# Operand places, turned maxima and the order of unfilled steps in an attention and MLP kernel

## The chip, the cores and the metric

The kernel runs on one core of a Trainium2 chip. The metric is the time of one execution in microseconds as the device reports it; lower is better. Before the change it is 1652.32 us, the median of three runs from 1651.63 to 1653.09.

A core has TensorE (matrix products, PE in the profile, with its weight loads as PEld), VectorE (DVE), ScalarE (ACT), GpSimd (POOL) and SyncE (SP, whose queue issues most of the DMAs). Each engine works through its own queue in order, and semaphores tie the queues together.

## The reference

One transformer block of 2048 rows and width 512, with adaptive layer norms. The attention has 32 heads of width 16, which share one key and one value head; the MLP has 1376 hidden columns. Cut to what matters:

```python
mod = (silu(c) @ w_mod).reshape(1, 6, 1, -1)          # sa, ca, ga, sb, cb, gb
h = layernorm(x) * (1 + ca) + sa
q = (h @ wq) as 32 heads;  k = h @ wk;  v = h @ wv
p = softmax(q @ k.T * 16 ** -0.5)                      # for each head
x = x + ga * (concat(p @ v) @ wo)
h = layernorm(x) * (1 + cb) + sb
x = x + gb * (gelu(h @ w1 + b1) @ w2 + b2)
```

## The kernel before

**Numbers.** Most products are float32r. To keep float32 accuracy, an operand is split into a high part and a low part (the rest), and a product is made of three: high by high, low by high, high by low. The helper `split` makes the parts, `mm3` and `batches` list the three products.

**Units and steps.** The rows are cut into eight blocks of 256, the heads into eight groups of four. A block and a group make a unit; there are 64. The keys are gone through 256 at a time: eight steps K for each unit. In a step, for the four heads of the unit,

- `Max.step` (L452) makes a score product m of 128 query rows by 512 keys, and VectorE reduces it to its maximum (L465). This runs about six steps ahead of the rest;
- `sexp` (L503) makes a score product e with keys on the rows. The maxima stand as two extra rows (48 and 49 of each half of qst, high and low part), so that the product has the maximum subtracted, and ScalarE takes the exponential into p (L516);
- `pv` (L518) multiplies p with the values and a column of ones into acc (L527), in four column tiles of the array at once.

The products m and e contract over 64 rows, so two run side by side, one in each half of the array: half s has rows 64 s to 64 s + 63.

**The maxima of a unit.** When the last m of a unit is reduced, VectorE reduces the four key chunks to mm, 128 rows by 8 (L473). Two quarters later `put_max` (L478) turns mm with a transpose on TensorE into the PSUM tile mt (L485), ScalarE copies it out (L489), GpSimd splits it into mh and ml, and two quarters after that four DMAs of SP put them into the rows of qst (L496).

**The order of the work** is written out by hand. Steps go in pairs X and Y, and a counter `clock` advances four quarters for each pair; `later(n, fn)` runs something n quarters on. Between the score products of a pair the kernel puts a batch of other products where one is ready (`take`): late query projections (qps), the output projection (wops), transposes (tp), the MLP (w1ps, w2ps). Its 64-row halves run in the half of the array that the scores leave free. A step with a batch is called filled here. Without a batch `plain` (L1248) issues the step alone, half of the m and e for each array half; `mixture` alternates two lists, and `issue` merges lists by their lengths. The loop is at L1230.

PSUM has eight banks: three for m, one each for e0, e1, e2, one (v) for acc, and one (x) for the batches.

```python
free = ((1, 2, 0, 1), (2, 0, 1, 2)) if holder else ((1, 2, 0, "x"), (1, 2, 0, "x"))
plain(1, X, 0, (n + 2) // 4, free[0])
```

The four numbers are the banks of the step's four e; `holder` is a batch job that still holds x.

**The late shift and scale columns.** The modulation rows for the second layer norm are made in the prologue as rows of a PSUM tile. `late_mods` (L873) sends two of them (ga, gb) to DRAM and back as rows for all partitions, and turns the two others (sb, cb) into columns with four TensorE transposes and two VectorE copies (L902 to L906).

**Places in SBUF.** `pad` (L84) allocates a small tile and zeroes it on GpSimd, so that what is allocated behind it lies further on. With the pads of this version, the operands of all float32r products start at multiples of 128 bytes in their partition: ks, qst, wqH, wqL, bigH, bigL, woH, woL, gH, gL, w1t and the tiles tagged xH and xL.

**The tail.** The last block's MLP has no attention beside it and uses the whole array (`fast`). `stir` (L680) issues products on ks there, whose result nobody reads, while the layer norm is made.

Of the kernel before, what the change touches and what calls it, by code (L numbers as in the profile page):

```python
# [15 lines left out]
P = 128  # L16
# [7 lines left out]
LEAD_0 = 3  # L24
QBUFS = 4
# [8 lines left out]
STIR = (4, 8, 4)  # L34
# [7 lines left out]
def adaln_mqa_mlp(  # L42
# [158 lines left out]
    xts = []  # L201

# [6 lines left out]
    pad(pro, 480, "pad1")  # L209
# [41 lines left out]
    pad(pro, 480, "pad2")  # L251
# [49 lines left out]

    wqH = att.tile([P, KD, D], F32R, name="wqH", tag="gH")
# [12 lines left out]
    hts_stats = {}  # L315
    bigH = att.tile([P, NB - 1, KD, BQ], F32R, name="bigH", tag="bigH")
# [4 lines left out]

    tps = {}
# [109 lines left out]
    class Max:  # L432
# [5 lines left out]
        def begin(self, u):  # L438
            T = blocks[units[u][0]][1] // P
            items = [(j, t, kc) for j in range(2) for t in range(T) for kc in range(NKC)]  # L440
            if u == 0:
                items.sort(key=lambda a: a[2])
            self.items[u] = [list(items), list(items)]
            self.left[u] = 2 * len(items)
            self.mx[u] = att.tile([P, 4 * T, NKC], F32, name=f"mx{u}", tag="mx", bufs=2)
            if u == 0:
                pad(att, 192, "pad3")
# [4 lines left out]
        def step(self, s):  # L452
# [9 lines left out]
            nc.tensor.matmul(m, qsts[u][rows, j, t * P:(t + 1) * P], ks[rows, kc * 512:(kc + 1) * 512],  # L462
                             start=True, stop=True)
            i = (s * 2 + j) * T + t
            nc.vector.tensor_reduce(out=self.mx[u][:, i, kc:kc + 1], in_=m, axis=AX.X, op=ALU.max)  # L465
            self.done += 1
            self.left[u] -= 1
            if self.left[u] == size[u] // 2 and u and u + 1 < NU:
                load_q(u + 1)
            if self.left[u] == 0:  # L470
                put_at[u] = clock[0] + 2
                mm = att.tile([P, 4 * T], F32, name=f"mm{u}", tag="mm", bufs=2)
                nc.vector.tensor_reduce(out=mm, in_=self.mx.pop(u), axis=AX.X, op=ALU.max)  # L473
                maxima[u] = mm

    maxima = {}

    def put_max(u):  # L478

        w = blocks[units[u][0]][1]  # L480
        T = w // P
        qst = qsts[u]
        mm = maxima.pop(u)
        pt = psum.tile([P, 512], F32, name=f"mt{u}", tag="m", bufs=3)
        nc.tensor.transpose(pt[:4 * T, :P], mm, ident)  # L485
        mh = att.tile([4 * T, P], F32R, name=f"mh{u}", tag="mh", bufs=2)
        ml = att.tile([4 * T, P], F32R, name=f"ml{u}", tag="ml", bufs=2)
        m32 = att.tile([4 * T, P], F32, name=f"m32_{u}", tag="m32", bufs=2)
        nc.scalar.copy(m32, pt[:4 * T, :P])  # L489
# [13 lines left out]
    def sexp(u, K, j, s, bank):  # L503

        w = blocks[units[u][0]][1]
        qst = qsts[u]
        if (u, K) not in ptiles:
# [7 lines left out]
        nc.tensor.matmul(e, ks[rows, kt * P:(kt + 1) * P], rhs, start=True, stop=True)  # L515
        nc.scalar.activation(ptiles[u, K][:, j, s, :], e, AF.Exp, scale=0.25)  # L516
# [163 lines left out]
    def stir(n):  # L680

        ps = psum.tile([P, BQ], F32, name=f"stir{len(idles)}", tag="x")
        idles.append(ps)
        for _ in range(n):
            nc.tensor.matmul(ps, ks[:, 0:P], ks[:, 0:BQ], start=True, stop=True)

    def rest_steps(b, fast, rp, bank, ons, ready):
# [6 lines left out]
        for hf in range(w // HQ):  # L694
# [37 lines left out]
            for t in range(2):  # L732
# [3 lines left out]
                if fast:  # L736
                    add_x(t, ps)
                    stats(t)
                    rstd(t, t + 1)
                    xhat(t)  # L740
                else:
                    add_x(t, ps)
                    later(2, lambda t=t: stats(t))
            if not fast:
                later(3, lambda: rstd(0, 2))
                later(4, lambda: xhat(0))
                later(4, lambda: xhat(1))
                yield 7
# [120 lines left out]
    drm = tc.dram_tile([2, D], F32, name="drm")  # L869
# [3 lines left out]
    def late_mods():  # L873
# [10 lines left out]
        def spread():  # L884
            nc.sync.dma_start(out=drm[0:1, :], in_=rows[0:1, :])
            nc.sync.dma_start(out=drm[1:2, :], in_=rows[96:97, :])
            later(3, collect)

        def collect():
            nc.sync.dma_start(out=ga, in_=drm[0:1, :].to_broadcast([P, D]))  # L890
            nc.sync.dma_start(out=gb, in_=drm[1:2, :].to_broadcast([P, D]))
            later(4, scale)

        def scale():
            nc.gpsimd.tensor_tensor(out=b2g, in0=b2r, in1=gb, op=ALU.mult)
# [4 lines left out]
        yield 4  # L900
        psc = psum.tile([P, KD, P], F32, name="modlc", tag="x")
        mod_cols(psc, rows, P)  # L902

        def cols():
            nc.vector.tensor_copy(out=sb, in_=psc[:, :, 32])
            nc.vector.tensor_scalar(out=cb1, in0=psc[:, :, 64], scalar1=1.0, scalar2=None, op0=ALU.add)  # L906

        yield 0
        cols()
# [29 lines left out]
    def prep_w1():  # L939
# [10 lines left out]
        def work(f):  # L950
            w1s[f] = rp.tile([P, 2, KD, P], F32R, name=f"w1s{f}", tag="w1t", bufs=3)
# [63 lines left out]
    put_at = {}  # L1015
# [162 lines left out]
    def put_some():  # L1178
        for u in sorted(maxima):
            if clock[0] >= put_at[u]:  # L1180
                put_max(u)

    while mp.done < lead[0]:
        if mp.done % 4 == 0:
            due()
            put_some()
# [7 lines left out]
    for u in sorted(maxima):  # L1194
        put_max(u)
# [24 lines left out]
    def end_step(u, K):  # L1220

        pv(u, K)
        put_some()
# [6 lines left out]
    for u in range(NU):  # L1230
        for K in range(0, steps[u], 2):
# [16 lines left out]
            def plain(s, K, t, n, banks):  # L1248

                a, b_, c_, d = banks  # L1250
                one = mixture(maxes(s, n), exps(s, [(K, 0, a), (K, 1, c_)]))
                other = maxes(t, n)
                issue(one, other[:1] + exps(t, [(K, 0, b_), (K, 1, d)]) + other[1:])
# [9 lines left out]
            else:  # L1263
                free = ((1, 2, 0, 1), (2, 0, 1, 2)) if holder else ((1, 2, 0, "x"), (1, 2, 0, "x"))
                plain(1, X, 0, (n + 2) // 4, free[0])
# [10 lines left out]
            else:  # L1276
                plain(1, Y, 0, n // 4, free[1])
# [68 lines left out]
```

## Time and profile before

| what | value |
|---|---|
| median of three runs | 1652.32 us (1651.63 to 1653.09) |
| profiled execution | 1652.47 us, its span 1650.6 us |
| TensorE products busy | 1613.0 us, 98% of the span |
| VectorE busy | 1418.4 us, 86% |
| ScalarE busy | 1222.8 us, 74% |
| GpSimd busy | 609.6 us, 37% |
| granted TensorE clock, mean | 0.997 |
| DMA | 22.3% of 16 engines for SP's queue |

The span is the time from the first to the last instruction in the trace. Busy time is the time in which an engine had at least one instruction running. TensorE's products overlap each other, so a product's own duration (about 0.39 us for 512 columns) is longer than the pitch at which products follow each other; where the text speaks of a pitch, it is the distance from start to start. In a row of groups the order is: line, engine, operation, out<-in with shapes, count, then busy us and mean ns of one, then the idle time of the engine just before and what ended it. In a timeline row it is: start in us, duration in us, engine, line, operation, tiles, count of merged instructions.

### The profile page before, as it was taken

The numbers are of one execution on the slowest core, as the hardware profiler recorded it, in microseconds if no ns is written. First come the engines' busy times: TensorE is split into PE (matmuls) and PEld (weight loads), VectorE is DVE, ScalarE is ACT, GpSimd is POOL, SyncE is SP. The second block draws the span as 40 slices with busy tenths as digits, with TensorE's granted clock in tenths as the row PEclk, the third lists the DMA queues.
The fourth block names the chain that finished last, engine by engine and source line by source line (L and its number), as shares of the span: only waits on it lengthen the run. The fifth ranks groups of instructions, "written<-read, shape, count | busy, mean of one in ns | idle before, by whom it ended". The sixth has DMA issues, their size and how long they took to land.

```text
span 1650.6 us, 41339 instructions
## 1 busy us (share of the span) xinstructions
PE 1613.0 (98%) x16387; PEld 1031.3 (62%) x16387; DVE 1418.4 (86%) x2433; ACT 1222.8 (74%) x2445; POOL 609.6 (37%) x898
## 2 busy tenths in 40 slices
PE   6999999999999999999999999999999999999998
PEld 4455644456666576656766576656766576656767
DVE  7688999999988998899988998899988998899625
ACT  4356777778877787778877787778877788778843
POOL 6235246424601363124601363124601364124613
PEclk9999999999999999999999999999999999999999
DMA  7234321212112030212112030122212030122232
GB/s 262 81 116 157 136 74 54 81 43 79 57 48 76 26 108 15 63 59 82 54 42 81 30 106 17 51 71 71 65 33 88 21 115 18 47 82 68 71 114 86
DMA packets 80157, 121.61 MB, mean 74 GB/s; under 512 B 15496, under 2 KB 53000, under 8 KB 79964
## 3 DMA queue, kind: packets, MB, share of 16 engines
q1 hardware_dynamic: 79852, 118.96, 22.3%
q8 instruction: 130, 2.13, 0.5%
q14 instruction: 63, 0.52, 0.1%
q0 software_dynamic: 112, 0.01, 0.0%
HBM read 91.13 MB, written 27.26 MB: 72 GB/s over the span
## 4 chain that ended last, share of the span: by engine, by line
PE 85%; DVE 9%; issue 2%; ACT 1%; POOL 1%; DMA 1%; SPq 1%; DVEq 0%; POOLq 0%; ACTq 0%
PE acc L527 29%; PE m L462 25%; PE e L515 14%; PE w1ps L177 6%; DVE mx L465 6%; PE w2ps L177 3%; PE wops L177 1%; PE w2ps L171 1%; PE w1ps L171 1%; ACT p L516 1%; PE mt L485 1%; PE kps L153 1%; PE qps L177 1%; PE tp L177 1%; DVE st L716 1%
## 5 line engine op out<-in xcount | busy, mean ns | idle before, releaser
L465 DVE TENSOR_REDUCE mx<-m 128x1 f32<-128x512 f32 x2048 | 1278.8, 682 | 150.1 <-PE m L462 121.9
L516 ACT ACTIVATE p<-e 128x512 f32<-128x512 f32 x2048 | 1071.3, 599 | 295.4 <-PE e L515 228.1
L462 PE MATMUL m<-ks,qst 64*128 64x512 f32 x2048 | 838.2, 433 | 12.1 <-DVE mx L465 4.1
L515 PE MATMUL e<-qst,ks 64*128 64x512 f32 x2048 | 704.1, 399 | 2.7 <-DMA qst<-ml 2.6
L527 PE MATMUL acc<-p,va 128*32 128x256 f32 x8192 | 548.0, 385 | 0.0
L462 PEld LDWEIGHTS m<-ks,qst 64*128 64x128 f32 x2048 | 358.7, 183 | 274.2 <-DVE mx L465 183.2
L515 PEld LDWEIGHTS e<-qst,ks 64*128 64x128 f32 x2048 | 359.6, 185 | 43.2 <-ACT p L516 19.1
L527 PEld LDWEIGHTS acc<-p,va 128*32 128x32 f32 x8192 | 213.8, 109 | 218.9 <-issue 117.1
L177 PE MATMUL w1ps<-h2H,w1t 64*128 64x256 f32 x1232 | 240.8, 290 | 0.0
L177 PEld LDWEIGHTS w1ps<-h2H,w1t 64*128 64x128 f32 x1232 | 186.5, 186 | 0.0
L123 POOL TENSOR_SCALAR mh<-m 8x128 fp32r<-8x128 f32 x64 | 18.5, 289 | 453.0 <-ACT m L489 446.0
L177 PE MATMUL w1ps<-h2L,w1t 64*128 64x256 f32 x616 | 171.8, 279 | 0.0
L177 PE MATMUL w2ps<-w2L,gH 64*128 64x512 f32 x282 | 115.7, 410 | 0.0
L177 PE MATMUL w2ps<-w2H,gH 64*128 64x512 f32 x282 | 115.5, 410 | 0.0
L177 PE MATMUL w2ps<-w2H,gL 64*128 64x512 f32 x282 | 115.5, 410 | 0.0
L177 PEld LDWEIGHTS w1ps<-h2L,w1t 64*128 64x128 f32 x616 | 114.8, 186 | 0.0
L811 POOL TENSOR_SCALAR tt<-tt 128x256 f32<-128x256 f32 x77 | 31.2, 405 | 179.6 <-DVE mx L465 98.5
L128 POOL TENSOR_TENSOR gL<-z,gH 128x256 fp32r<-128x256 f32 x88 | 66.3, 753 | 18.2 <-DVE gH L127 11.8
L812 POOL TENSOR_TENSOR tt<-tt,z 128x256 f32<-128x256 f32 x77 | 56.9, 739 | 6.4
L822 POOL TENSOR_TENSOR z<-tt,z 128x256 f32<-128x256 f32 x77 | 56.1, 729 | 6.0
L821 POOL TENSOR_TENSOR tt<-tt,z 128x256 f32<-128x256 f32 x77 | 56.2, 730 | 0.0
L177 PEld LDWEIGHTS w2ps<-w2H,gH 64*128 64x128 f32 x282 | 51.9, 184 | 0.6
(186 smaller groups left out, 1445.8 us busy)
## 6 DMA issues: line engine op xcount, KB each, us to landing
w1t<-dw SPq DMA_DIRECT2D x82, 512.0 KB
qst<-dq SPq DMA_DIRECT2D x384, 32.0 KB
do<-oc SPq DMA_DIRECT2D x64, 128.0 KB
dw<-w1s SPq DMA_DIRECT2D x11, 512.0 KB
xt<-in_A_x_dram SPq DMA_DIRECT2D x4, 1024.0 KB
wml<-in_w_mod_dram SPq DMA_DIRECT2D x8, 512.0 KB
dq<-qH SPq DMA_DIRECT2D x16, 256.0 KB
dq<-qL SPq DMA_DIRECT2D x16, 256.0 KB
```

The costliest lines, as they stand in the source:

```text
L128: eng_l.tensor_tensor(out=dst_l, in0=src, in1=raw(dst_h), op=ALU.subtract)
L171: nc.tensor.matmul(ps, a, b_, start=first_, stop=last_)
L177: nc.tensor.matmul(ps, a[rows], b_[rows], start=first_ and s == 0, stop=last_ and s == 1)
L462: nc.tensor.matmul(m, qsts[u][rows, j, t * P:(t + 1) * P], ks[rows, kc * 512:(kc + 1) * 512], start=True, stop=True)
L465: nc.vector.tensor_reduce(out=self.mx[u][:, i, kc:kc + 1], in_=m, axis=AX.X, op=ALU.max)
L515: nc.tensor.matmul(e, ks[rows, kt * P:(kt + 1) * P], rhs, start=True, stop=True)
L516: nc.scalar.activation(ptiles[u, K][:, j, s, :], e, AF.Exp, scale=0.25)
L527: nc.tensor.matmul(accs[u][32 * cidx:32 * cidx + 32, :], va[:, kt, :], rhs, start=kt == 0, stop=kt == NKT - 1)
L811: nc.gpsimd.tensor_scalar(out=tt, in0=tt, scalar1=1.0, scalar2=1.0, op0=ALU.mult, op1=ALU.add)
L812: nc.gpsimd.tensor_tensor(out=tt, in0=tt, in1=z, op=ALU.mult)
L821: nc.gpsimd.tensor_tensor(out=tt, in0=tt, in1=z, op=ALU.mult)
L822: nc.gpsimd.tensor_tensor(out=z, in0=tt, in1=z, op=ALU.add)
```

## The change

- **Places.** Pads of 64 bytes go before xt and p (and with them qst), before wqH, before bigH, before the tiles xH and xL, and before w1t. After that, in each float32r product, one operand starts at a multiple of 128 bytes and the other 64 bytes past one. Two later pads keep what follows in place.
- **Maxima.** `put_max` runs at once when a unit's last m is reduced. VectorE reduces into one of two fixed tiles of 128 by 32 (zeroed once) and turns it in 32 by 32 blocks. One quarter later GpSimd copies the four pieces of 8 by 32 into mt, 8 by 128, and splits it; four quarters after the maximum the four DMAs are issued. The transpose on TensorE and ScalarE's copy are gone.
- **Order.** In an unfilled step, e goes first in both halves, and the fourth m is written to the bank x where no batch holds it. The four e use only e0 to e2, so that the fourth has the bank of the first.
- **Columns.** sb and cb go to DRAM as rows and come back as columns by DMA, with GpSimd adding one. The four transposes and two copies of `late_mods`, and its two waits, are gone.
- **Smaller.** In the blocks that are not the last, the layer norm's statistics and what follows run one quarter later. `stir` issues the same number of products, with the moving operand starting at columns 0, 4, 8 and so on.

```diff
-STIR = (4, 8, 4)
+STIR = ((0, 0, 0, 0), (0, 4, 8, 12, 16, 20, 24, 28), (16, 32, 48, 0))
+MAX_WAIT = (1, 4)
...
+    pad(att, 64, "pad1")
     def load_x(b):
...
+    pad(att, 64, "pad4")
     wqH = att.tile([P, KD, D], F32R, name="wqH", tag="gH")
...
+    pad(att, 64, "pad5")
     bigH = att.tile([P, NB - 1, KD, BQ], F32R, name="bigH", tag="bigH")
...
+    pad(att, 64, "pad6")
     tps = {}
...
-            m = psum.tile([P, 512], F32, name=f"m{u}_{j}_{t}_{kc}_{s}", tag="m", bufs=3)
+            m = psum.tile([P, 512], F32, name=f"m{u}_{j}_{t}_{kc}_{s}", **(place or dict(tag="m", bufs=3)))
...
             if self.left[u] == 0:
-                put_at[u] = clock[0] + 2
-                mm = att.tile([P, 4 * T], F32, name=f"mm{u}", tag="mm", bufs=2)
-                nc.vector.tensor_reduce(out=mm, in_=self.mx.pop(u), axis=AX.X, op=ALU.max)
-                maxima[u] = mm
+                put_max(u, self.mx.pop(u))
...
-        pt = psum.tile([P, 512], F32, name=f"mt{u}", tag="m", bufs=3)
-        nc.tensor.transpose(pt[:4 * T, :P], mm, ident)
...
-        nc.scalar.copy(m32, pt[:4 * T, :P])
-        split(mh, ml, m32, nc.gpsimd, nc.gpsimd)
+        nc.vector.tensor_reduce(out=mm[:, :4 * T], in_=mx, axis=AX.X, op=ALU.max)
+        turned = att.tile([P, 32], F32, name=f"turned{u}", tag="turned", bufs=2)
+        nc.vector.transpose(out=turned, in_=mm)
+        mt = att.tile([4 * T, P], F32, name=f"mt{u}", tag="mt", bufs=2)
...
-        later(2, send)
+        def gather():
+            for g in range(0, P, 32):
+                nc.gpsimd.tensor_scalar(out=mt[:, g:g + 32], in0=turned[g:g + 4 * T, :], scalar1=1.0, scalar2=0.0,
+                                        op0=ALU.mult, op1=ALU.add)
+            split(mh, ml, mt, nc.gpsimd, nc.gpsimd)
+
+        later(MAX_WAIT[0], gather)
+        later(MAX_WAIT[1], send)
...
         def spread():
             nc.sync.dma_start(out=drm[0:1, :], in_=rows[0:1, :])
             nc.sync.dma_start(out=drm[1:2, :], in_=rows[96:97, :])
+            nc.sync.dma_start(out=drm[2:3, :], in_=rows[32:33, :])
+            nc.sync.dma_start(out=drm[3:4, :], in_=rows[64:65, :])
...
+                nc.sync.dma_start(out=sb, in_=drm[2].rearrange("(k p) -> p k", p=P))
+                nc.sync.dma_start(out=cb1, in_=drm[3].rearrange("(k p) -> p k", p=P))
...
-        psc = psum.tile([P, KD, P], F32, name="modlc", tag="x")
-        mod_cols(psc, rows, P)
...
+            if f == 0:
+                pad(rp, 64, "pad8")
...
-                one = mixture(maxes(s, n), exps(s, [(K, 0, a), (K, 1, c_)]))
+                one = mixture(exps(s, [(K, 0, a), (K, 1, c_)]), maxes(s, n))
                 other = maxes(t, n)
-                issue(one, other[:1] + exps(t, [(K, 0, b_), (K, 1, d)]) + other[1:])
+                if not holder and mp.has(t) and n > 1:
+                    other[-1] = 1.0, lambda: mp.step(t, tag="x", bufs=1)
+                issue(one, exps(t, [(K, 0, b_)]) + other + exps(t, [(K, 1, d)]))
...
-                free = ((1, 2, 0, 1), (2, 0, 1, 2)) if holder else ((1, 2, 0, "x"), (1, 2, 0, "x"))
-                plain(1, X, 0, (n + 2) // 4, free[0])
+                plain(1, X, 0, (n + 2) // 4, (1, 2, 0, 1))
...
-                    later(2, lambda t=t: stats(t))
+                    later(3, lambda t=t: stats(t))
```

More of the change, by code (lines that the diff above doesn't have):

```diff
@@ L506, in sexp @@
         qst = qsts[u]
+        assert u in placed
         if (u, K) not in ptiles:
@@ L678, in fetch_rest, with stir @@
         early[b] = x1, w1ts
-    def stir(n):
+    def stir(starts):
         ps = psum.tile([P, BQ], F32, name=f"stir{len(idles)}", tag="x")
         idles.append(ps)
-        for _ in range(n):
-            nc.tensor.matmul(ps, ks[:, 0:P], ks[:, 0:BQ], start=True, stop=True)
+        for i in starts:
+            nc.tensor.matmul(ps, ks[:, 0:P], ks[:, i:i + BQ], start=True, stop=True)
     def rest_steps(b, fast, rp, bank, ons, ready):
@@ L742, in rest_steps @@
                     add_x(t, ps)
-                    later(2, lambda t=t: stats(t))
+                    later(3, lambda t=t: stats(t))
             if not fast:
[L745 to L748, printed above, removed]
+                later(4, lambda: rstd(0, 2))
+                later(5, lambda: xhat(0))
+                later(5, lambda: xhat(1))
+                yield 8
             hH = att.tile([P, KD, HQ], F32R, name=f"h2H{b}_{hf}", tag="xH", bufs=2)
@@ L1193, in adaln_mqa_mlp @@
             clock[0] += 1
-    for u in sorted(maxima):
-        put_max(u)
     preps["w1"] = prep_w1()
```

45 lines of the change are left out of this document (19 added, 26 removed).

## The prediction

> **What bounds the kernel now.** I read the page first: the busy shares, the chain that ended last, the dearest groups.
>
> ```profile
> span 1650.6 us, 41339 instructions
> PE 1613.0 (98%) x16387; PEld 1031.3 (62%) x16387; DVE 1418.4 (86%) x2433; ACT 1222.8 (74%) x2445; POOL 609.6 (37%) x898
> PE 85%; DVE 9%; issue 2%; ACT 1%; POOL 1%; DMA 1%; SPq 1%; DVEq 0%; POOLq 0%; ACTq 0%
> L465 DVE TENSOR_REDUCE mx<-m 128x1 f32<-128x512 f32 x2048 | 1278.8, 682 | 150.1 <-PE m L462 121.9
> L516 ACT ACTIVATE p<-e 128x512 f32<-128x512 f32 x2048 | 1071.3, 599 | 295.4 <-PE e L515 228.1
> ```
>
> TensorE carries 85% of the chain. VectorE, second, is idle mostly because it waits for m: it follows TensorE, not the reverse. The profiled execution took 1652.47 us (1.9 around its span of 1650.6), beside a median of 1652.32, so the sum below holds for the median too.
>
> The attention loop has 64 units of eight key steps, and 512 steps fill nearly the whole span. There are two kinds. A filled step carries a batch of projection or MLP products on one half of the array while the other half does m and e. An unfilled one has m and e alone. How many there are follows from the groups, with shapes kept apart:
>
> ```profile
> L177 PE MATMUL w1ps<-h2H,w1t 64*128 64x256 f32 x1232 | 240.8, 290 | 0.0
> L177 PE MATMUL w1ps<-h2L,w1t 64*128 64x256 f32 x616 | 171.8, 279 | 0.0
> L177 PE MATMUL w2ps<-w2L,gH 64*128 64x512 f32 x282 | 115.7, 410 | 0.0
> L177 PE MATMUL wops<-woL,onH 64*128 64x512 f32 x112 | 43.8, 391 | 0.0
> L177 PE MATMUL tp<-ident,xh 64*128 64x128 f32 x224 | 32.1, 284 | 0.0
> L177 PE MATMUL qps<-bigL,wqH 64*128 64x512 f32 x72 | 28.3, 393 | 0.0
> ```
>
> A w1 step has 12 half products: 1848 / 12 = 154 steps. The w2, wo and qps rows stand three times each (high·high, low·high, high·low): 846 / 5.5 = 154, 336 / 6 = 56, 216 / 6 = 36. tp has eight records a step: 28. That is 428 filled steps, and 84 unfilled.
>
> One filled step, TensorE in order of time (start, us, and what; the rows left out alternate m and e, with w1 products between):
>
> ```profile
> 800.79 1.07 PE L527 MATMUL acc<-p,va 128*32 128x256 f32 x16
> 801.79 0.49 PE L462 MATMUL m<-ks,qst 64*128 64x512 f32 x1
> ...
> 802.13 0.39 PE L515 MATMUL e<-qst,ks 64*128 64x512 f32 x1
> ...
> 803.29 0.42 PE L462 MATMUL m<-ks,qst 64*128 64x512 f32 x1
> ...
> 803.65 1.07 PE L527 MATMUL acc<-p,va 128*32 128x256 f32 x16
> ```
>
> The step takes 803.65 − 800.79 = 2.86 us: 1.00 for acc, 0.34 to the second product, five pitches of (803.29 − 802.13) / 5 = 0.232, and 0.36 until acc can start. No gap waits for anything: this step is as long as its products' pitch makes it.
>
> An unfilled stretch, TensorE, then VectorE and ScalarE in the same stretch:
>
> ```profile
> 250.85 1.07 PE L527 MATMUL acc<-p,va 128*32 128x256 f32 x16
> 251.85 0.27 PE L485 MATMUL mt<-ident,mm 128*8 128x128 f32 x1
> 252.06 0.66 PE L462 MATMUL m<-ks,qst 64*128 64x512 f32 x2
> ...
> 253.76 1.07 PE L527 MATMUL acc<-p,va 128*32 128x256 f32 x16
> 254.77 0.50 PE L462 MATMUL m<-ks,qst 64*128 64x512 f32 x2
> 255.10 0.39 PE L515 MATMUL e<-qst,ks 64*128 64x512 f32 x2
> ...
> 256.05 0.50 PE L462 MATMUL m<-ks,qst 64*128 64x512 f32 x1
> 256.48 1.07 PE L527 MATMUL acc<-p,va 128*32 128x256 f32 x16
> ```
>
> ```profile
> 255.30 2.48 DVE L465 TENSOR_REDUCE mx<-m 128x1 f32<-128x512 f32 x4 [0.23 <-PE m L462]
> ```
>
> ```profile
> 255.53 2.07 ACT L516 ACTIVATE p<-e 128x512 f32<-128x512 f32 x4 [0.64 <-PE e L515]
> ```
>
> Here the step is 256.48 − 253.76 = 2.72, although it has far less to do. m has three PSUM buffers, so its fourth product waits for the first reduction: 255.30 + 0.68 = 255.98, and m starts at 256.05. Only then can acc go. VectorE's own need is smaller: four reductions take 2.48, a pitch of (2.48 − 0.68) / 3 = 0.60, so 2.40 a step.
>
> **The change, part by part.**
>
> *The turned maxima.* Removed from TensorE: 64 transposes mt. From acc to the next m it is 252.06 − 250.85 = 1.21 with one and 254.77 − 253.76 = 1.01 without: 0.20 each, on the chain in both kinds of step. 64 × 0.20 = 12.8; I take 12, since the first lies in the prologue and a little may return. VectorE gets a 32x32-block transpose of 128x32, in its queue right behind the last reduction. Nearest row:
>
> ```profile
> L473 DVE TENSOR_REDUCE mm<-mx 128x8 f32<-128x32 f32 x64 | 11.9, 186 | 2.2
> L123 POOL TENSOR_SCALAR mh<-m 8x128 fp32r<-8x128 f32 x64 | 18.5, 289 | 453.0 <-ACT m L489 446.0
> L128 POOL TENSOR_TENSOR ml<-m,mh 8x128 fp32r<-8x128 f32 x64 | 29.0, 452 | 5.3
> ```
>
> About 0.19, 12 us in all, covered by VectorE's idle 0.23 before a step's m. Without that cover it would be up to 0.19 × 64 = 12 and the saving would be gone; what queues behind it are the next reductions, for which TensorE's next m waits. ScalarE loses a small copy each time. GpSimd gets four copies of 8x32, each at most 0.29 by the mh row: 1.16 more a unit, 74 us on top of 609.6 of 1650.6, off the chain. Should GpSimd be late, the sends of the rows wait in SP's queue, and everything SP issues behind them. The gather is issued one quarter of a step pair after the maximum (before: at the end of a later step), the four sends four quarters after it, about one quarter earlier than now. They pass no load that a product needs at once; priced at 0. mm now comes from two fixed tiles, zeroed once.
>
> *Order of unfilled steps.* e goes first, and the last m takes a fourth buffer, x, where no batch holds it. Then no m waits. But the fourth e now reuses the bank of the first e, and waits for its exponential. A first product after acc reaches its reader 255.30 − 254.77 = 0.53 later; the exponential is 0.60, the restart 0.07: 1.20, against 256.05 − 254.77 = 1.28 now. 0.08 × 84 = 7 us. Bounds: VectorE's 2.40 would allow 2.72 − 2.40 = 0.32 × 84 = 27; and 0, or a small loss, if ScalarE has an oc copy or a tanh in front. I take 7, because the new wait is a row of the same stretch.
>
> *The 64 bytes.* In the layout of before, both operands of every fp32r product start at a multiple of 128 bytes. Five pads of 64 bytes put one of the two at 64. No fp32r product in this trace lies otherwise, so the rows can only bound it. From the tail, whole array, no waits:
>
> ```profile
> 1596.12 0.39 PE L171 MATMUL w2ps<-w2L,gH 128*128 128x512 f32 x1
> ...
> 1602.92 0.39 PE L171 MATMUL w2ps<-w2L,gH 128*128 128x512 f32 x1
> ...
> 1609.50 0.60 PE L769 MATMUL tp<-ident,xh 128*128 128x128 f32 x4
> ```
>
> ```profile
> 1617.39 0.28 PE L171 MATMUL w1ps<-h2L,w1t 128*128 128x256 f32 x1
> ...
> 1621.70 0.28 PE L171 MATMUL w1ps<-h2L,w1t 128*128 128x256 f32 x1
> ```
>
> 512 columns: (1602.92 − 1596.12) / 30 = 0.2267. 256 columns: 4.31 / 36 = 0.1197. The difference, 0.107 for 256 columns, is the streaming; so each product has 0.013 added whatever its width, and in the half array 0.232 − 0.214 = 0.018. The addition belongs to the weight load, not to the streaming. Yet the fp32 transposes load 128 columns too, at (0.60 − 0.27) / 3 = 0.11 for 128 columns streamed at half the rate, which is the streaming alone. So it looks like two reads that collide only when the moving operand is read at full rate; where they lie relative to each other could then matter. Ends: 0; all of it, 0.016 a pitch (0.232 to 0.216); and, as nothing excludes the other sign, the same addition once more, 0.013 lost. I take a gain of 0.010, nearer to the transposes' row than to 0. A filled step has six such pitches on its chain: 0.06 × 428 = 26; nine tenths of it, 23, since VectorE is close by in the w1 stretch (53.16 busy of 58 us):
>
> ```profile
> 383.00:441.00 58.00, 58.00 (x720) 41.29 (x717) 53.16 (x93) 49.66 (x105) 36.44 (x62) 1.00 0.28 88
> ```
>
> The tail has some 260 such products: 2.6; the prologue gives about 1. Together 27.
>
> The Trainium skill says otherwise: its page "TensorE: Matmul & The Clock Gate", section "Step-by-step: what each phase is for", gives weights and moving operand a read port each, so that loading the next weights takes nothing from the running matmul. By that the 64 bytes give 0 and the sum is 1633. The trace doesn't bear the page's whole account out: its section "Back-to-back issue gap" states N/2.4 + 2.5 ns, which would be an estimated 215.8 for 512 columns where these rows have 226.7.
>
> *The rest.* The shift columns by DMA: two more writes and two loads in SP's queue, once, ahead of the second unit's four sends; four transposes and two small VectorE copies go, and the queue of batches moves up. Bounds −2 to +2; 0 taken. stats, rstd and xhat one quarter of a step pair later in seven blocks: the unfilled steps behind them cover it; without that, seven quarters of 1.4, 10 us. Pads: small memsets on GpSimd before the loop, 0. stir: 16 products as before, 0. Filled steps keep their order.
>
> Sum: 1652.5 − 12 − 7 − 27 = 1606.5, said as 1606.
>
> **Rivals.** (1) The 64 bytes do nothing: the addition is a fixed cost of a weight load. For it: it is the same 13 ns at both widths; against: the transposes lack it. 1652.5 − 19 = 1633. The Trainium skill's page named above is on this side. (2) The 64 bytes hurt: 0.013 more on each pitch, six in each of 428 steps and 260 in the tail: 2828 × 0.013 = 37, less 19: 1670. It decides from 19 / 2828 = 0.007 a pitch. For it: only that no row shows the sign. (3) Nothing from the 64 bytes, and VectorE's turn is paid in full: it stands between two reductions while the m buffers are full, so that TensorE waits 0.19 for its next m, 64 times, 12 us. 1633 + 12 = 1645; with 0.3 a turn, 1652 and no change. VectorE's idle before m speaks against it.
>
> **How the numbers follow.** Forecast (1590 to 1625, as the gain is 0.016 or a third of that) 0.46; rival 1 0.27; rival 2 0.17; rival 3 0.10, of which 0.06 counts as no change and 0.04 as faster. About 0.2%, 3 us, can be told from no change. Faster 0.46 + 0.27 + 0.04 = 0.77, same 0.06, slower 0.17. The range goes from 1585 (full gain, and part of the 27 in unfilled steps) to 1650, which leaves out rival 2 and the worse part of 3.
>
> **What would show it.** Tail w2 products at a pitch under 0.222 (right) or at 0.227 and above (rivals 1, 2); stir, whose moving operand starts at several offsets, would show the pitch for each. acc to m at 1.01 everywhere, no mt. Unfilled steps at 2.63, fourth e waiting for p. VectorE's wait for m shorter, TensorE's for mx not longer. If the tail's pitch is unchanged, the term of 27 is wrong; if unfilled steps stay at 2.7, the term of 7.

## The result, and the profile after

The kernel after takes 1629.75 us (median; 1627.34 to 1631.07) beside 1652.46 for the kernel before: a ratio of 0.9861, with a 95% interval of 0.9844 to 0.9878. That is 23.0 us faster; the forecast was 46. The profiled execution took 1627.34, of which the span is 1625.5. (Below, a gain in us is 1652.5 times what the ratio of that run lacks to 1.)

The page of the kernel after: span, busy shares, the chain that ended last, then three of its dearest groups (out<-in, count, busy us and mean ns, idle before it and what ended most of it).

```profile
span 1625.5 us, 41474 instructions
PE 1594.2 (98%) x16319; PEld 1028.4 (63%) x16319; DVE 1426.0 (88%) x2495; ACT 1207.1 (74%) x2381; POOL 664.6 (41%) x1162
PE 81%; DVE 8%; issue 3%; POOL 2%; DMA 1%; ACT 0%; SPq 0%; POOLq 0%; DVEq 0%
L468 DVE TENSOR_REDUCE mx<-m 128x1 f32<-128x512 f32 x2048 | 1274.3, 682 | 115.2 <-PE m L465 88.9
L465 PEld LDWEIGHTS m<-ks,qst 64*128 64x128 f32 x2048 | 357.6, 184 | 229.4 <-DVE mx L468 141.5
L531 PEld LDWEIGHTS e<-qst,ks 64*128 64x128 f32 x2048 | 362.1, 184 | 91.3 <-ACT p L532 67.8
```

The same two rows of weight loads on the page of the kernel before:

```profile
L462 PEld LDWEIGHTS m<-ks,qst 64*128 64x128 f32 x2048 | 358.7, 183 | 274.2 <-DVE mx L465 183.2
L515 PEld LDWEIGHTS e<-qst,ks 64*128 64x128 f32 x2048 | 359.6, 185 | 43.2 <-ACT p L516 19.1
```

TensorE's weight loads (PEld) wait 42 us less for VectorE (183.2 to 141.5) ahead of m, and 49 more for ScalarE ahead of e (19.1 to 67.8): the new wait of the fourth e, which the prediction had named. VectorE still has 8% of the chain.

Three stretches of TensorE in the kernel after. First an unfilled step:

```profile
526.79 1.07 PE L543 MATMUL acc<-p,va 128*32 128x256 f32 x16
527.79 0.50 PE L531 MATMUL e<-qst,ks 64*128 64x512 f32 x2
...
528.97 0.50 PE L531 MATMUL e<-qst,ks 64*128 64x512 f32 x1
529.40 1.07 PE L543 MATMUL acc<-p,va 128*32 128x256 f32 x16
```

and the weight load of its last e:

```profile
528.97 0.18 PEld L531 LDWEIGHTS e<-qst,ks 64*128 64x128 f32 x1 [0.31 <-ACT p L532]
```

529.40 − 526.79 = 2.61, where the prediction had 2.63, and the last product ahead of acc is now an e, which waits for ScalarE's p. Then the tail's products, whole array, 512 columns and 256:

```profile
1572.30 0.39 PE L172 MATMUL w2ps<-w2L,gH 128*128 128x512 f32 x1
...
1577.80 0.39 PE L172 MATMUL w2ps<-w2L,gH 128*128 128x512 f32 x1
...
1594.02 0.28 PE L172 MATMUL w1ps<-h2L,w1t 128*128 128x256 f32 x1
...
1606.26 0.28 PE L172 MATMUL w1ps<-h2L,w1t 128*128 128x256 f32 x1
```

24 products of 512 columns lie between the first two rows: 5.50 / 24 = 0.229, against 0.2267 before. 108 of 256 columns lie between the last two: 12.24 / 108 = 0.1133, against 0.1197. So the long products are a little slower and the short ones faster. The prediction had set its own test: a w2 pitch of 0.227 or more means that the term of 27 is wrong. The other sign that it named says the same: stir's products, with the moving operand at several offsets, follow each other at 226 to 237 ns in the kernel after (224 to 236 before, from one place), but for the first two of a later burst.

The steps of the loop, from one acc to the next, summed by what they are filled with (worked out from the starts of acc in the two traces):

| steps | before, us | after, us |
|---|---|---|
| unfilled, 83 | 231.9 | 219.9 |
| w1, 154 | 451.0 | 447.5 |
| w2, 154 | 445.3 | 442.0 |
| qps, 36 (before: one with the shift columns) | 114.5 | 111.7 |
| wo, 56 | 168.7 | 166.0 |
| tp, 28 | 83.2 | 84.7 |

More than half of the gain lies in the unfilled steps. The w1 and w2 steps, 308 of the 428 filled ones, lose 6.8 together, where by the prediction's 0.06 a step and its nine tenths 17 of the 27 should have appeared. The tp steps have become longer, which the prediction did not have.

### The profile page after: what moved, and what is told of

Its sections match the earlier page's. It is cut to its first block, busy times and chain, and to the rows that moved or that the text cites. A ratio compares the mean times of both kernels' runs of the same rounds, so it can differ in the third digit from the quotient of the medians.

```text
span 1625.5 us, 41474 instructions
## 1 busy us (share of the span) xinstructions
PE 1594.2 (98%) x16319; PEld 1028.4 (63%) x16319; DVE 1426.0 (88%) x2495; ACT 1207.1 (74%) x2381; POOL 664.6 (41%) x1162
## 4 chain that ended last, share of the span: by engine, by line
PE 81%; DVE 8%; issue 3%; POOL 2%; DMA 1%; ACT 0%; SPq 0%; POOLq 0%; DVEq 0%
PE acc L543 28%; PE m L465 22%; PE e L531 17%; PE w1ps L178 7%; DVE mx L468 6%; PE w2ps L178 3%; PE wops L178 2%; PE w2ps L172 1%; PE w1ps L172 1%; PE tp L178 1%; PE qps L178 1%; POOL qL L129 0%; DMA os<-drs 0%; POOL w1s L129 0%; DVE st L732 0%
## 5 line engine op out<-in xcount | busy, mean ns | idle before, releaser
L465 PE MATMUL m<-ks,qst 64*128 64x512 f32 x2048 | 804.9, 424 | 6.5 <-DVE mx L468 3.0
L531 PE MATMUL e<-qst,ks 64*128 64x512 f32 x2048 | 745.5, 411 | 1.9 <-DMA qst<-ml 1.7
L465 PEld LDWEIGHTS m<-ks,qst 64*128 64x128 f32 x2048 | 357.6, 184 | 229.4 <-DVE mx L468 141.5
L531 PEld LDWEIGHTS e<-qst,ks 64*128 64x128 f32 x2048 | 362.1, 184 | 91.3 <-ACT p L532 67.8
L178 PE MATMUL w1ps<-h2H,w1t 64*128 64x256 f32 x1232 | 235.3, 287 | 0.0
L508 POOL TENSOR_SCALAR mt<-turned 8x32 f32<-8x32 f32 x256 | 53.5, 209 | 389.3 <-DVE turned L494 247.5
L178 PE MATMUL w2ps<-w2L,gH 64*128 64x512 f32 x282 | 115.6, 410 | 0.0
L670 POOL TENSOR_TENSOR os<-os 128x256 f32<-128x256 f32 x28 | 20.6, 736 | 82.3 <-DMA os<-drs 81.0
```

The costliest lines, as they stand in the source:

```text
L178: nc.tensor.matmul(ps, a[rows], b_[rows], start=first_ and s == 0, stop=last_ and s == 1)
L508: nc.gpsimd.tensor_scalar(out=mt[:, g:g + 32], in0=turned[g:g + 4 * T, :], scalar1=1.0, scalar2=0.0, op0=ALU.mult, op1=ALU.add)
```

## The experiments

The first four kernels ran on one chip; each gain here is taken against the kernel before on the same chip. The four split the change: one takes the five pads out of the kernel after, three add one part to the kernel before.

**Without the 64 bytes.** The edit, five times:

```diff
-    pad(att, 64, "pad1")
```

> The kernel after, without its five pads of 64 bytes. The forecast's theory (the two reads of a product collide unless they lie 64 bytes apart, 27 us): the time goes back by 23 to 27, to some 1654. Rival A (the 64 bytes act on the 256-column products alone, whose pitch went from 120.0 to 113.4 ns in the whole array, and little of that is on the path): 1630 to 1634, and the 256-column pitch is 120 again. Rival B (nothing at all): 1629 to 1631, with the 256-column pitch still at 113.

Measured: 1633.68, ratio 0.9884 [0.9870, 0.9897], a gain of 19.2: the pads are worth 3.8 of the 23.0. The mean pitch of the tail's products is back at 119.9 ns (256 columns) and 227 (512).

**The 64 bytes alone.** Five pads at the places that the kernel after has, of which this is the first:

```diff
+    pad(att, 64, "padA")
...
```

> The kernel before with nothing but the five pads of 64 bytes. The forecast's theory: 1652.5 less 27, 1625. Rival A: 1648 to 1653, the 256-column pitch of the tail at 113 to 114 ns and the 512-column pitch at 227 or a little more. Rival B: 1652, pitches of 120 and 227.

Measured: 1648.21, ratio 0.9975 [0.9964, 0.9985], a gain of 4.1. The mean pitches in the tail are 113.4 and 229.2 ns. In the loop the w1 steps lose 3.2 us together (451.0 to 447.8) and the w2 steps 0.9. Rival A of the expectations holds from both sides: with and without the other parts, the 64 bytes give 4, and mainly in the steps whose products have 256 columns.

**The turn alone**: VectorE's transpose and GpSimd's copies in place of TensorE's transpose, in the kernel before.

```diff
-        nc.tensor.transpose(pt[:4 * T, :P], mm, ident)
...
-        nc.scalar.copy(m32, pt[:4 * T, :P])
...
+        nc.vector.transpose(out=turned, in_=mm)
...
+            for g in range(0, P, 32):
+                nc.gpsimd.tensor_scalar(out=mt[:, g:g + 32], in0=turned[g:g + 4 * T, :], scalar1=1.0, scalar2=0.0,
+                                        op0=ALU.mult, op1=ALU.add)
...
```

> The kernel before with nothing but the new way of turning the maxima (VectorE turns them, GpSimd arranges them, no TensorE transpose). The prediction's term: 12 us less, 1640, as 64 steps lose 0.20 each. If VectorE's turn were paid in full, 1645 to 1652.

Measured: 1649.09, ratio 0.9976 [0.9967, 0.9985], a gain of 4.0, a third of the 12. No step has an mt any more, and the 63 steps that had one are 0.20 shorter on the mean, 12.8 us together; but the steps in which the maximum and the turn now stand, mostly just ahead of those (every eighth step, 64 in all), are longer: 191.04 us together became 198.67. The turn gives 7.6 of the 12.8 back. In the w1 stretch, by place in the unit, the mean of a step went from 3.06 to 2.86 for the step with mt and from 2.93 to 3.05 for the one ahead of it. Here is such a step ahead. VectorE, before:

```profile
406.64 0.47 DVE L806 TENSOR_SCALAR z<-w1ps,b1c 128x256 f32<-128x256 f32 x1
407.03 0.68 DVE L465 TENSOR_REDUCE mx<-m 128x1 f32<-128x512 f32 x1
407.75 0.19 DVE L473 TENSOR_REDUCE mm<-mx 128x8 f32<-128x32 f32 x1
407.85 2.47 DVE L465 TENSOR_REDUCE mx<-m 128x1 f32<-128x512 f32 x4
```

and the same step with the turn alone, VectorE, then the end of the step on TensorE:

```profile
407.67 0.48 DVE L818 TENSOR_SCALAR z<-w1ps,b1c 128x256 f32<-128x256 f32 x1
408.06 0.68 DVE L464 TENSOR_REDUCE mx<-m 128x1 f32<-128x512 f32 x1
408.77 0.19 DVE L486 TENSOR_REDUCE mm<-mx 128x8 f32<-128x32 f32 x1
408.99 0.21 DVE L490 STREAM_TRANSPOSE turned<-mm 128x32 f32<-128x32 f32 x1
409.13 2.44 DVE L464 TENSOR_REDUCE mx<-m 128x1 f32<-128x512 f32 x4
```

```profile
409.83 0.50 PE L461 MATMUL m<-ks,qst 64*128 64x512 f32 x1
410.26 0.42 PE L539 MATMUL acc<-p,va 128*32 128x256 f32 x4
```

From mm to the next reduction it is 0.10 before (407.75 to 407.85) and 0.36 with the turn (408.77 to 409.13): the turn costs 0.26, since it cannot start until mm is written. The first of the four reductions ends at 409.13 + 0.68 = 409.81, and at 409.83 the last m takes its buffer: it has waited, and acc behind it. In this step a z also stands ahead of the maximum, so the cover that the prediction counted on, VectorE's 0.23 of idle time, isn't there. Over all 64 units the median from the start of mm to the next reduction is 0.10 before and 0.36 with the turn.

**The order of unfilled steps alone.**

```diff
-                one = mixture(maxes(s, n), exps(s, [(K, 0, a), (K, 1, c_)]))
+                one = mixture(exps(s, [(K, 0, a), (K, 1, c_)]), maxes(s, n))
...
-                issue(one, other[:1] + exps(t, [(K, 0, b_), (K, 1, d)]) + other[1:])
+                if not holder and mp.has(t) and n > 1:
+                    other[-1] = 1.0, lambda: mp.step(t, tag="x", bufs=1)
+                issue(one, exps(t, [(K, 0, b_)]) + other + exps(t, [(K, 1, d)]))
...
-                plain(1, X, 0, (n + 2) // 4, free[0])
+                plain(1, X, 0, (n + 2) // 4, (1, 2, 0, 1))
...
```

> The kernel before with nothing but the order of unfilled steps (exp products first, the last m in a fourth buffer). The prediction's term: 7 us less, 1645, with unfilled steps at 2.63 instead of 2.72. From the sums of steps of the kernel after (unfilled steps 12 us shorter in all, of which a part belongs to the turned maxima): 1642 to 1647.

Measured: 1638.76, ratio 0.9914 [0.9900, 0.9927], a gain of 14.2, twice the term of 7. The usual step went from 2.71 to 2.61, which over some 73 steps is 7 and what was forecast. Another 5.5 comes from seven steps, one in each block, that went from 3.39 to 2.61, and 1.5 from two steps with six m and a single other one. Before, such a step, TensorE, then VectorE:

```profile
535.27 1.07 PE L527 MATMUL acc<-p,va 128*32 128x256 f32 x16
...
538.23 0.49 PE L462 MATMUL m<-ks,qst 64*128 64x512 f32 x1 [0.47 <-DVE mx L465]
538.65 0.42 PE L527 MATMUL acc<-p,va 128*32 128x256 f32 x4
```

```profile
535.71 0.68 DVE L709 TENSOR_TENSOR x<-wops,x 128x512 f32<-128x512 f32 x1
536.31 0.68 DVE L465 TENSOR_REDUCE mx<-m 128x1 f32<-128x512 f32 x1
536.91 0.68 DVE L716 BATCH_NORM_STATS2 st<-x 128x6 f32<-128x512 f32 x1
537.51 1.87 DVE L465 TENSOR_REDUCE mx<-m 128x1 f32<-128x512 f32 x3
```

The residual sum and the norm's statistics stand ahead of the reduction that the fourth m waits for. With a fourth buffer m needs no reduction of its own step, so what VectorE does there no longer reaches TensorE in that step. The edit changes two things, the order of e and m and the bank of the fourth m, and no run has one without the other. The same place with the order alone:

```profile
529.41 1.07 PE L527 MATMUL acc<-p,va 128*32 128x256 f32 x16
...
531.60 0.50 PE L515 MATMUL e<-qst,ks 64*128 64x512 f32 x1
532.03 0.42 PE L527 MATMUL acc<-p,va 128*32 128x256 f32 x4
```

**The turn behind the next step's reductions.** In the kernel after, the maximum and the turn of each unit are put off by three quarters of a step pair.

```diff
-MAX_WAIT = (1, 4)
+MAX_WAIT = (1, 2)
+TURN_WAIT = 3
...
-                put_max(u, self.mx.pop(u))
+                later(TURN_WAIT, lambda mx=self.mx.pop(u): put_max(u, mx))
```

> The kernel after, with the maximum of a unit and VectorE's turn put behind the four reductions of the next step instead of ahead of them (gather and sends follow one and two quarters of a step pair later). Theory P (the turn is paid: it stands ahead of four reductions for which TensorE's m waits, 0.12 to 0.3 us in the step behind each unit's last m; behind them VectorE has its idle time while acc runs): these 63 steps lose 0.1 to 0.15 each, the tp steps 0.4, together 6 to 9: 1621 to 1624. Theory H (the turn costs nothing, other work makes those steps longer): 1629 to 1630, the steps unchanged. Theory S (it is paid wherever it stands, since VectorE has no idle time to give): the time moves to the step behind, 1629 to 1630.

Measured: 1625.74, ratio 0.9834 [0.9820, 0.9849], 4.5 faster than the kernel after and between the ranges of the theories. By the traces, the steps behind a unit's last m (every eighth, 64 in all) fell from 198.25 to 186.26 us, 12.0 together. But steps 7, 15 and 16 took 7.8 back: there the rows of units 1 and 2 now came late. Both the maximum's reduction and the turn have moved here, 0.19 and 0.21 of VectorE's time, so the 12.0 is the price of the two at that place; the turn by itself had made these steps 7.6 longer in the kernel before. The tp step shows the effect most plainly. VectorE and TensorE in the kernel after:

```profile
530.94 5.46 DVE L468 TENSOR_REDUCE mx<-m 128x1 f32<-128x512 f32 x9
536.43 0.19 DVE L490 TENSOR_REDUCE mm<-mx 128x8 f32<-128x32 f32 x1
536.73 0.21 DVE L494 STREAM_TRANSPOSE turned<-mm 128x32 f32<-128x32 f32 x1
536.86 1.84 DVE L468 TENSOR_REDUCE mx<-m 128x1 f32<-128x512 f32 x3
```

```profile
534.71 1.07 PE L543 MATMUL acc<-p,va 128*32 128x256 f32 x16
...
537.57 0.50 PE L465 MATMUL m<-ks,qst 64*128 64x512 f32 x1 [0.20 <-DVE mx L468]
...
538.00 0.42 PE L543 MATMUL acc<-p,va 128*32 128x256 f32 x4
```

Nine reductions stand back to back: with four buffers the unfilled steps ahead run at VectorE's expense, and leave it a backlog. Then mm and the turn, and the m that waits for the first reduction behind them starts at 537.57, right behind its end (536.86 + 0.68). Filled steps have three m buffers, as before. The step takes 3.29; with the order alone it took 2.95 on the mean, with the turn alone 2.91, before 2.85: each eats a part of the same slack.

**The turn twice.** A second VectorE transpose into a tile that nobody reads.

```diff
...
         nc.vector.transpose(out=turned, in_=mm)
+        nc.vector.transpose(out=twice, in_=mm)
```

The pad behind these tiles is smaller by the new tile's 128 bytes.

> The kernel after, with VectorE's turn of each unit made twice, the second into a tile that nobody reads. Theory P: the first turn has used up what cover there was, so 0.15 to 0.27 more in each of 63 steps, 9 to 17: 1639 to 1647. Theory H: 1629 to 1631.

Measured: 1635.59, ratio 0.9893 [0.9878, 0.9908], 5.3 slower than the kernel after. The same 64 steps went from 198.25 to 202.40, 4.15 of the 5.3; w1 ones went from 3.07 to 3.16. VectorE's time at this place is paid, so theory H falls; but 0.09 a step is less than the 0.15 to 0.27 expected. VectorE, in a w1 step:

```profile
402.16 0.21 DVE L495 STREAM_TRANSPOSE turned<-mm 128x32 f32<-128x32 f32 x1
402.30 0.17 DVE L496 STREAM_TRANSPOSE twice<-mm 128x32 f32<-128x32 f32 x1
402.39 1.84 DVE L468 TENSOR_REDUCE mx<-m 128x1 f32<-128x512 f32 x3
```

The second turn, which needn't wait for mm, holds the queue for 402.39 − 402.30 = 0.09, and that is what the w1 steps became longer by.

**Stats where they were.**

```diff
-                    later(3, lambda t=t: stats(t))
+                    later(2, lambda t=t: stats(t))
```

(and rstd, xhat and the yield likewise, each by one)

> The kernel after, with stats, rstd and xhat of seven blocks where they were before, one quarter of a step pair earlier. The wo steps that lost 0.3 to 0.6 each (3.61 and 3.90 to 3.31, one in each block) get it back, 2 to 4 us: 1632 to 1634. If the tp steps (2.85 to 3.28, one in each block) have become longer by this move, they get shorter by 0.3 each, and the two cancel: 1629 to 1631. The prediction took the move at 0.

Measured: 1632.68, ratio 0.9873 [0.9857, 0.9890]. The wo steps get 3.4 back (165.97 to 169.36; the one that also ends a unit goes from 3.31 to 3.90 in each block), and the tp steps stay at 84.5: they have not become longer by this move. The ratios make the move worth 2.0, with some 4 either way, and so do not tell it from 0; the wo steps, which show it in every block, say 3.4.

**The pitch by place.** In the kernel before, products were added in an idle stretch of the tail; nobody reads them. i counts numbers of 4 bytes, eight products for each value. The kernel ran once, in 1781.42 us; only its trace is used.

```diff
+                for i in list(range(33)) + [48, 64]:
...
+                        nc.tensor.matmul(ps[:, :N], ks[:, 0:P], ks[:, i:i + N], start=True, stop=True)
...
+                for cols in (32, 64, 96, 128):
...
+                        nc.tensor.matmul(ps[:cols, :N], ks[:, 0:cols], ks[:, 0:N], start=True, stop=True)
...
```

> The kernel before, with float32r products of the whole array added to the second idle stretch of the tail, weights and moving operand from the same tile: first the moving operand's start shifted by 0 to 32 and by 48 and 64 numbers of 4 bytes against the weights', eight products each, 512 and 256 columns; then weights 32, 64, 96 and 128 columns wide; then the weights' start shifted. The forecast's theory (two reads collide at equal places): 226.7 ns at a distance of 0 and of 128 bytes, 214 to 220 at 64. Rival A (a short product's addition depends on the place, a long one's doesn't): 512 columns 227 to 231 everywhere, 256 columns 120 at 0 and 113 at 64. Rival B (a fixed cost of a weight load): the same at every distance; if the cost is that of loading columns, narrower weights shrink it in proportion, and if it is a fixed restart, not.

The groups by line of that kernel, shapes kept apart (tile size as rows*columns of the array, count, busy us, mean ns):

```profile
L690 PE MATMUL stir<-ks 128*128 128x512 f32 x280 | 65.2, 394 | 0.0
L690 PE MATMUL stir<-ks 128*128 128x256 f32 x280 | 33.5, 282 | 0.0
```

Over all 35 distances the mean is 65.2 / 280 = 0.233 and 33.5 / 280 = 0.120. By distance, the mean of seven intervals, in ns, from the starts in the trace:

| distance, bytes | 512 columns | 256 columns |
|---|---|---|
| 0 | 228.1 | 118.9 |
| 16 | 231.0 | 113.3 |
| 32 | 233.1 | 117.3 |
| 64 | 228.4 | 118.1 |
| 128 | 233.3 | 119.7 |
| all, 4 modulo 16 (8 distances) | 233.6 to 237.6 | 118.4 to 122.6 |
| all, 12 modulo 16 (8 distances) | 227.4 to 232.3 | 115.6 to 120.1 |
| lowest and highest of all 35 | 227.4, 239.3 | 113.3, 122.6 |

No distance brings a product of 512 columns near the 214 of pure streaming, and 64 bytes is no better than 0. Shifting the weights' start instead, by 0 to 112 bytes, gave 226.7 to 233.9 and 114.0 to 119.4. The weights' width does not matter either: 32 to 128 columns gave 231.7, 229.1, 231.4 and 227.1. How far such a mean of seven can be trusted is shown by three groups at distance 0 with 128 columns of weights: 228.1, 227.1 and 230.6.

The forecast's theory falls here by itself. At every place a product takes longer than the streaming that the prediction read from its rows (0.214 and 0.107), by 13 to 25 ns for 512 columns and 6 to 16 for 256. What this addition is isn't settled; a cost in proportion to the columns loaded is excluded. Rival A's 113 at 64 bytes did not come either: the map has 118.1 there, where the pads gave 113.4 to w1's two tiles, so the distance of the two operands is not the whole rule for short products.

The Trainium skill, "TensorE: Matmul & The Clock Gate", section "Step-by-step: what each phase is for", has separate read ports for weights and moving operand; that no place should matter then is what the prediction made of it. The tail's 119.9 without and 113.4 with the pads differs from that; for 512 columns, which decide here, it was much nearer to the truth than the forecast.

**The later turn, without the late rows.** Two runs were to leave the early units as they were. The first did it through the list of postponed work, which issued their maxima one quarter late all the same.

```diff
-                put_max(u, self.mx.pop(u))
+                later(3 if u > 3 else 0, lambda mx=self.mx.pop(u): put_max(u, mx))
...
-        later(MAX_WAIT[1], send)
+        later(2 if u > 3 else MAX_WAIT[1], send)
```

> The kernel after, with the turn behind the next step's reductions (as in the run with the later turn) from unit 4 on alone; units 0 to 3, whose rows are needed soonest, keep the turn and the sends where the kernel after has them. Theory P with what the later turn showed (the 63 steps behind a unit's last maximum lost 12 us in all, and three steps of the first units, which waited for the rows, took 7.8 back): 1629.75 - 12 + 1 = 1617 to 1620. Theory H or S: 1629, as the sums would only have moved.

Measured: 1624.20, ratio 0.9833 [0.9820, 0.9847]: no better than putting off all, which missed the expectation. The reason is one row of TensorE in step 7:

```profile
114.79 0.49 PE L465 MATMUL m<-ks,qst 64*128 64x512 f32 x1
117.62 0.46 PE L531 MATMUL e<-qst,ks 64*128 64x512 f32 x1 [2.35 <-DMA qst<-ml]
```

The rows of the first units have no quarter to spare. So, with a direct call for them:

```diff
-                put_max(u, self.mx.pop(u))
+                if u < 4:
+                    put_max(u, self.mx.pop(u))
+                else:
+                    later(3, lambda mx=self.mx.pop(u): put_max(u, mx))
...
-        later(MAX_WAIT[1], send)
+        later(2 if u > 3 else MAX_WAIT[1], send)
```

> As the run before it (turn behind the next step's reductions from unit 4 on), but units 0 to 3 now keep the turn, the gather and the sends exactly where the kernel after has them; in the run before they came one quarter of a step pair later, and steps 7 and 15 waited 2.35 us and more for the rows of units 1 and 2, 5.8 in all. Theory P: 1629.75 less 12.3 in the steps behind a unit's last maximum, and 2 or so given back in the steps where the turn now stands: 1618 to 1621, steps 7 and 15 at 4.0 and 4.5. Theory S: 1624 or more again.

Measured: 1618.93, ratio 0.9799 [0.9785, 0.9812]: 33.2 faster than the kernel before, 10.2 faster than the kernel after. Steps 7 and 15 are at 3.99 and 4.46. The 64 steps are at 185.98, and the tp step of the same block:

```profile
532.05 1.07 PE L546 MATMUL acc<-p,va 128*32 128x256 f32 x16
...
534.89 0.64 PE L546 MATMUL acc<-p,va 128*32 128x256 f32 x8
```

```profile
530.66 5.47 DVE L468 TENSOR_REDUCE mx<-m 128x1 f32<-128x512 f32 x9
536.04 0.18 DVE L493 TENSOR_REDUCE mm<-mx 128x8 f32<-128x32 f32 x1
```

The nine reductions are there as in the kernel after, but the maximum comes when the step is over (acc at 534.89, mm at 536.04). The step takes 2.84. On the page, the share of VectorE in the chain has halved:

```profile
PE 85%; DVE 4%; issue 3%; POOL 2%; DMA 1%; ACT 0%; SPq 0%; POOLq 0%; DVEq 0%
```

**Earlier sends for the first units**, to win what steps 7 and 15 wait; the edit against the run just told.

```diff
-        later(2 if u > 3 else MAX_WAIT[1], send)
+        later(2, send)
```

> The same with the sends of units 0 to 3 two quarters earlier, one quarter behind the gather. If steps 7 and 15 (4.0 and 4.5 in the kernel after, 2.9 and 3.3 without a wait) wait for the place of the sends in the issue order: 2 less, 1616 to 1619. If they wait for GpSimd's arranging of the rows or for the transfers themselves: no change.

Measured: 1618.98, ratio 0.9796 [0.9783, 0.9810], steps 7 and 15 at 4.00 and 4.47: no change. The place of the sends in the issue order isn't what these steps wait for. GpSimd's copies and splits, which stand behind its q work, or the transfers themselves are left. For step 15 there is one thing more: with the shift columns back on TensorE (the next run) it takes 3.39. There step 8 is 1.76 longer, which gives the rows that much more time, and the columns' transfers are gone from SP's queue; no run separates the two.

**The shift columns on TensorE, as before**, in the kernel after.

```diff
-                nc.sync.dma_start(out=sb, in_=drm[2].rearrange("(k p) -> p k", p=P))
...
+        psc = psum.tile([P, KD, P], F32, name="modlc", tag="x")
+        mod_cols(psc, rows, P)
...
```

> The kernel after, with the shift columns turned by TensorE and copied by VectorE, as before. The prediction's 0, with ends of 2: 1628 to 1632. In the trace of the kernel after, a step of 4.66 had become 2.90 where the transposes had stood, and one of 2.71 had become 4.51 later; if both belong to the columns, the two cancel; if only the first does, 1631.5.

Measured: 1632.12, ratio 0.9871 [0.9857, 0.9885]. The interval overlaps that of the kernel after, so this part of the change is not told from 0. Its step of 4.66 us is back, and two other qps steps (13 and 15) are 1.7 shorter in exchange. The step that had become 4.51 stays: it has nothing to do with the columns.

## Why the prediction was half right

The direction was right, and the time lies in the range (1585 to 1650), but the gain was half of what was forecast: 1629.75 lies outside the 1590 to 1625 that the forecast gave its own theory, and nearer to rival 1's 1633 than to 1606. By terms:

| term | forecast, us | measured alone, us | 95% |
|---|---|---|---|
| 64-byte places | 27 | 4.1 | 2.5 to 5.9 |
| turned maxima | 12 | 4.0 | 2.5 to 5.5 |
| order of unfilled steps | 7 | 14.2 | 12.1 to 16.5 |
| stats later | 0 | 2.0 (difference of two ratios) | not told from 0 |
| shift columns | 0 | 1.7 (the same) | not told from 0 |

The middle values add to 26, beside a measured 23.0 with an interval of 20.2 to 25.8.

*The 64 bytes* are the step that failed: the gain of 0.010 on each pitch, from a collision of two reads that no row of the kernel before showed. The prediction saw that every float32r product has 0.013 added, and that the fp32 transposes lack it, and wrote: "So it looks like two reads that collide only when the moving operand is read at full rate; where they lie relative to each other could then matter." It took 0.010 a pitch, nearer to the transposes' row than to 0. Measured, the 512-column pitch of the tail went up by 0.002, not down, and in the map no distance helps it. The transposes' row was no evidence of a collision: they differ from the float32r products in type and in rate, and no row has the same product with its operands in another place. Why they lack the addition stays open; that slow streaming hides it is not enough, as their 0.11 is about the 0.107 in which a 256-column product streams, and that product has it. The 256-column products did gain 0.0065 in the tail, but a w1 step is not made of these alone: m and e run in the other half of the array, with 512 columns, and from the second product of a w1 step to the seventh their pitch is 0.233 before and 0.232 with the 64 bytes alone. So the 154 w1 steps lost 3.2, about 0.02 each. On this term rival 1 was right, up to 4 us.

*The turn*: the saving on TensorE was right to the hundredth (0.20, the mean of the 63 steps that had an mt). What failed is its cover, "covered by VectorE's idle 0.23 before a step's m". This 0.23 was a row of an unfilled step without a maximum. Where the turn stands, mm has just run ahead of it, and in w1 steps z as well, so the step ahead became longer, by 0.13 in the w1 stretch and by up to 0.29 elsewhere (wo). This is the mechanism of rival 3, priced there at 0.19 a unit. It is shown three times: doubling the turn costs 5.3, moving it behind the reductions, together with the maximum, gives 10.2, and the steps where the time goes and comes back are those behind a unit's last m.

*The order*: the fourth e does wait for p, and the step is 2.61 for a forecast of 2.63. The size was off because the term was taken from the common step alone. Seven steps with other work on VectorE gained 0.78 each, as that work is off TensorE's path there too. Part of it is given back in the tp steps, by VectorE's backlog.

*stats one quarter later* was taken as covered, 0; by the steps it took 3.4 us out of the wo steps, which the ratios do not tell from 0.

So the failures had both signs, and that the time lies in the range is luck in part: 23 too much for the places, 8 too much for the turn, 7 too little for the order, and perhaps 2 each for stats and columns.

## What to carry to other kernels

When work is moved onto an engine, ask where in that engine's queue it lands and what else stands there in that step; idle time seen in another kind of step is no cover. Here 0.4 us of VectorE work a unit, the maximum and its turn, cost 10 us more ahead of four reductions than behind them. And before a fixed addition to every instruction is put down to an alignment, look for a row in which the place differs, or measure the pitch by place first.

## What the hardware showed that was not expected

- A float32r product with its own weight load takes 227 to 239 ns for 512 columns and 113 to 123 ns for 256, whatever the distance of its two operands in the map, and whether 32 or 128 columns of weights are loaded. The start modulo 16 bytes seems to matter more than modulo 128: on the mean, starts 4 bytes behind a multiple of 16 were slowest (235.7 and 120.8 ns) and those 12 behind fastest (229.3 and 117.6). Eight products for each place in one run are little for a rule.
- The same five pads make short products faster (119.9 to 113.4 ns) and long ones slower (227 to 229). They are not the whole rule: with all five in, the tail's short products are at 118 ns in the runs with the turn later and the turn twice, whose tiles are allocated otherwise.
- VectorE's 128x32 transpose takes 0.21 us, but holds its queue for 0.26 where it follows the instruction that writes its input; a second one right behind it, which waits for nothing, 0.09.
- An order that frees TensorE of a wait for VectorE doesn't make VectorE faster: it leaves a backlog, which is paid by the next step that has one buffer less (nine reductions back to back, and a tp step of 3.29 for 2.85).
